# Two token tiles normalised before their transpose, and the order of the early work written as a table

## The chip, the cores and the metric

The kernel runs on one NeuronCore of a Trainium2 chip. The metric is the device time of one execution in microseconds (us). The engines work side by side and each goes through its own list of instructions in order: PE (TensorE, matmuls and transposes; PEld is its weight load), DVE (VectorE), ACT (ScalarE, activations), POOL (GpSimd) and SP (SyncE), which here issues nearly all the DMAs. An instruction that depends on another engine waits on a semaphore, and what is queued behind it on its own engine waits with it.

## The reference

The input x has 2048 tokens of 512 features, all tensors are bf16. Two residual blocks follow one another:

```
h  = x + A(layernorm(x));   out = h + B(layernorm(h))
A: q, k, v = x @ wqkv, 32 heads of 16;  phi(t) = (t + 1 if t > 0 else exp(t)) + 1e-6
   kv = sum_s phi(k) v;  z = sum_s phi(k);  o = phi(q) kv / (phi(q) z + 1e-6);  return o @ wo
B: z = gelu(x @ w_in);  z1, z2 = halves of z, 896 each;  z2 = layernorm(z2)
   g = w_sp @ z2 + b_sp   (2048 x 2048 mix over tokens);   return (z1 * g) @ w_out
layernorm(t) = (t - mean) / sqrt(var + 1e-5)
```

## The kernel before, in words

Tokens are cut into 16 tiles n = 0..15 of 128. The early stage, which the change touches, does this for each tile (lines of the profile in brackets). SP loads x[n] (L540). DVE takes mean and variance (`st`, L590, and `ag`, L594). ACT computes the reciprocal standard deviation as Ln (L605) and then Exp (L607); the groups in `LN1` (L418) share one such pair, so that tiles 2 and 3 have one pair, 4 to 7 one, and so on. The normalised tile xn[n] is written by DVE (L617) or, for tiles 5, 7, 9, 11, 13, 15, by ACT (L625). xn has to be transposed to feed the matmuls: tiles 2 and 3 go through PE (L635) and an ACT copy (L701), tiles 4 to 15 through a transposing DMA issued by SP (`tx`, L675).

Tiles 0 and 1 (`LATE`, L414) take another way. DVE subtracts only the mean into a copy `xc` (L657), PE transposes that (L686), ACT and DVE copy one half each out of PSUM (L691, L693), the k matmuls read this centred x^T (L747), and the missing factor is applied in `phi` as the scale operand of the Exp and the Relu (L716, L722). Their xn is made as well (L617), since the product xk = xn^T phi(k) reads it (L768), and a transposing DMA (L695) puts it into x^T for the q matmuls (L860).

Then `phi` of k: Exp on ACT (L716), minimum on DVE (L718), Relu on ACT (L722), sum on DVE (L724); for q, the last two are one DVE instruction (L727) that reads PSUM. PSUM has eight banks of which four hold xk until the end of the stage, so that two tiles of two banks each are left for k and q: a matmul that needs such a tile waits for the last reader of the one before. After this stage come the mixing matrix of A (to about 55 us), the output of A, the layernorm of h, z2 (L968), z1 (L1023), the token mix (L1063) and the last projection (L1083).

What sets the order: every operation is declared in `build` with `op(engine, cost, function, reads, writes, want)` and gets a number in order of declaration. `schedule` (L151) plans them with modelled costs: for each engine it takes, among the operations whose inputs are planned, the one with the smallest time plus half its `want`, from the list `WANT` (L359). The order found is the order in which the engine's instructions are emitted (`run`, L345). `fillers` (L1108) puts dummy matmuls (L578) in front of PE operations wherever the plan shows PE idle, up to the first xk. Before that, eight of them are the operation `spin` (L585).

One operation on ACT has no reader and no input: line 572, named "table".

```
op("act", (0.1, 1.3), lambda e: e.preload_act_table_set("natural_log_exp_and_others"), want=-40, name="table")
```

It loads a set of ACT's function tables by name. Nothing in the kernel loads any other set; the Gelu of line 975 has no such operation of its own.

Of the kernel before, what the change touches and what calls it, by code (L numbers as in the profile page):

```python
# [6 lines left out]
BF16 = mybir.dt.bfloat16  # L7
# [6 lines left out]
SWITCH = 0.1  # L14

# [77 lines left out]
class Program:  # L93
# [3 lines left out]
    WEIGHT = 0.5  # L97
# [53 lines left out]
    def schedule(self):  # L151

        for o in self.ops:
            o.start = None
# [5 lines left out]
        users, need = {}, {}  # L160
        for o in self.ops:
            need[o] = len(o.deps)
            for p in o.deps:
                users.setdefault(p, []).append(o)
        cand = {e: [] for e in self.ENGINES}
        for o in self.ops:
            if not need[o]:
                cand[o.eng].append(o)
        free = dict.fromkeys(self.ENGINES, 0.85)
        order = {e: [] for e in self.ENGINES}  # L170
        c_end, t_end, left, last, ring, tiling = 0.0, -9.0, len(self.ops), None, [], 0
# [21 lines left out]
        while left:  # L193
            pick = None
            for e in self.ENGINES:
                best = None
                for o in cand[e]:
                    t = free[e] + (SWITCH if e == "pe" and o.tiling != tiling else 0.0)
                    for p in o.deps:
                        t = max(t, self.ready(o, e, p))  # L200
                    ok = True
                    for tl in o.tiles:
                        if tl.slot is None:
                            s = slot(tl)
                            if s is None:
                                ok = False
                                break
                            t = max(t, s[0])
                    if ok:
                        key = (t + self.WEIGHT * o.want, o.seq)  # L210
                        if best is None or key < best[0]:
                            best = (key, o, t)
                if best is not None and (pick is None or best[2] < pick[2]):
                    pick = best
            assert pick is not None, ("no operation can go on", [(e, [(o.name, [(t.pool.name, t.width) for t in o.tiles if t.slot is None]) for o in cand[e]][:6]) for e in self.ENGINES], [(p.name, [t.ops[0].name for t in p.tiles if t.slot is not None and t.left]) for p in self.pools])
            _, o, t = pick
# [12 lines left out]
            if o.grp is not None:  # L229
                if o.nbytes < 0:  # L230
                    if len(ring) >= 3:
                        free[o.eng] = max(free[o.eng], ring[-3] - 0.3)
                    t_end = max(t + 2.2, t_end + 0.48, c_end + 0.45)
                    ring.append(t_end)
                    o.done = t_end + 0.3
                else:
                    c_end = max(t + 1.5, c_end, t_end + 1.2)
                    k = min(o.nbytes, max(0.0, 6.2 - c_end) * 250e3)
                    c_end += k / 250e3 + (o.nbytes - k) / 350e3
                    o.done = c_end + 0.4  # L240
# [7 lines left out]
            o.pos = len(order[o.eng])  # L248
# [5 lines left out]
            order[o.eng].append(o)  # L254
            cand[o.eng].remove(o)
            for u in users.get(o, ()):
                need[u] -= 1
                if not need[u]:
                    cand[u.eng].append(u)
            left -= 1  # L260
        self.order = order
# [96 lines left out]
UNIT = 0.1  # L358
WANT = [  # L359
# [37 lines left out]
]  # L397


def build(nc, A_x, A_wqkv, A_wo, B_w_in, B_w_sp, B_b_sp, B_w_out, out):  # L400
    _, S, D = A_x.shape
    F = B_w_in.shape[1]
    FH = F // 2
    H, DH = 32, D // 32
    GW = 512
    NT, KD, KF, NG = S // P, D // P, FH // P, S // GW
    TPG = GW // P
    NP = NT // 2
# [780 lines left out]
```

## Time and profile before

| | us |
|---|---|
| three timed runs | 241.86, 242.42, 245.08 (median 242.42) |
| span of the profiled execution | 240.8 |
| PE busy in the span | 235.3 |
| DVE, ACT, POOL busy | 127.1, 83.9, 13.9 |
| dummy matmuls of line 578 | 12, from 0.8 to 9.2 us |
| ACT table loads | 2, each 1.28 (at 0.79 and at 59.50) |

The profiled execution is described by its span, from its first to its last instruction. Its own time isn't listed apart; the fastest timed run lies 1.06 above that span and the median 1.62 above it. In a row of the timeline the first number is the start, the second the length, then engine, line, operation, and behind "x" how many instructions are merged into the row; the bracket tells the idle time of the engine before it and what ended it. The end of a matmul is modelled, so that rows of PE can overlap by some tenths.

### The profile page before, as it was taken

What the parts mean: (1) busy time and instruction counts of PE and PEld (TensorE: products, weight loads), DVE (VectorE), ACT (ScalarE), POOL (GpSimd) and SP (SyncE); (2) the same over time, 40 slices, a digit from 0 to 9 for tenths busy, and PEclk for the clock granted to TensorE, in tenths of its full rate; (3) what the DMA queues carried; (4) which work ended last, traced back from release to release, by engine and by line L of the source; (5) the groups of instructions that cost most, each with busy time, mean ns of one, the idle gap of its engine ahead of it and who ended that gap; (6) DMA issues with size and microseconds to landing.
All of it is one profiled execution on the core that took longest, in us unless ns stands there. A gap on an engine that the chain in (4) does not pass through costs nothing.

```text
span 240.8 us, 3056 instructions
## 1 busy us (share of the span) xinstructions
PE 235.3 (98%) x1177; PEld 108.4 (45%) x1199; DVE 127.1 (53%) x269; ACT 83.9 (35%) x132; POOL 13.9 (6%) x33
## 2 busy tenths in 40 slices
PE   8999999999999999999999999999999999999996
PEld 2434445454344544444444444444444444444443
DVE  4999856399999983226222333324333433322443
ACT  4888975566065799994111100000000000000000
POOL 3000000000102160213000000000000000000000
PEclk9999999999999999999999999999999999999999
DMA  6986559632542555444444449463300001000022
GB/s 197 254 224 91 109 114 355 207 112 81 145 125 44 92 107 101 97 88 89 109 92 104 88 92 237 108 89 88 109 0 0 25 22 44 0 3 0 0 87 87
DMA packets 61805, 24.18 MB, mean 100 GB/s; under 512 B 52064, under 2 KB 61152, under 8 KB 61792
## 3 DMA queue, kind: packets, MB, share of 16 engines
q1 hardware_dynamic: 61648, 23.97, 41.3%
q8 instruction: 9, 0.15, 0.3%
q10 hardware_dynamic: 144, 0.03, 0.1%
q14 instruction: 4, 0.03, 0.1%
HBM read 7.47 MB, written 2.10 MB: 40 GB/s over the span
## 4 chain that ended last, share of the span: by engine, by line
PE 87%; DMA 5%; DVE 3%; ACT 2%; SPq 1%; issue 1%; ACTq 0%
PE ps L1063 40%; PE ps L1083 10%; PE ps L968 10%; PE ps L1023 10%; PE ps L768 4%; PE ps L860 4%; DMA xT_pq_z<-k_xn_z 4%; PE ps L905 3%; PE ps L758 3%; PE ps L578 2%; DMA wsp<-e 1%; ACT e L716 1%; SPq L886 1%; DVE xT_pq_z L727 1%; ACT k_xn_z L836 1%
## 5 line engine op out<-in xcount | busy, mean ns | idle before, releaser
L1063 PE MATMUL ps<-wsp,k_xn_z 128*128 128x512 bf16 x328 | 73.6, 379 | 0.4
L1069 DVE TENSOR_TENSOR e<-ps,e 128x512 bf16<-128x512 f32 x28 | 19.4, 692 | 69.2 <-PE ps L1063 69.2
L1063 PEld LDWEIGHTS ps<-wsp,k_xn_z 128*128 128x128 bf16 x336 | 32.8, 98 | 39.8 <-issue 0.4
L1023 PE MATMUL ps<-hT,win 128*128 128x512 bf16 x110 | 26.0, 379 | 0.1
L968 PE MATMUL ps<-win,hT 128*128 128x384 bf16 (+1 forms) x126 | 25.3, 352 | 0.1
L1083 PE MATMUL ps<-wout,xT_pq_z 128*128 128x512 bf16 (+2 forms) x125 | 25.1, 355 | 0.1
L1063 PE MATMUL ps<-wqkv_wsp,k_xn_z 128*128 128x512 bf16 x110 | 24.2, 379 | 0.1
L1028 ACT ACTIVATE xT_pq_z<-ps 128x1024 bf16<-128x1024 f32 x14 | 14.1, 1023 | 25.6 <-PE ps L1023 25.5
L590 DVE BATCH_NORM_STATS2 small<-xh 128x6 f32<-128x512 bf16 x32 | 21.0, 679 | 3.1 <-DMA xh<-in_A_x_dram 3.0
L968 PEld LDWEIGHTS ps<-win,hT 128*128 128x128 bf16 x128 | 12.5, 98 | 12.4
L1083 PEld LDWEIGHTS ps<-wout,xT_pq_z 128*128 128x128 bf16 x126 | 11.8, 98 | 12.7
L1063 PEld LDWEIGHTS ps<-wqkv_wsp,k_xn_z 128*128 128x128 bf16 x112 | 11.0, 98 | 13.2
L1023 PEld LDWEIGHTS ps<-hT,win 128*128 128x128 bf16 x112 | 10.9, 98 | 12.7 <-DVE xh L924 0.3
L1087 DVE TENSOR_TENSOR e<-ps,xh 128x512 bf16<-128x512 f32 (+2 forms) x18 | 11.4, 633 | 9.7 <-PE ps L1083 9.2
L716 ACT ACTIVATE e<-ps 128x1024 bf16<-128x1024 f32 (+1 forms) x16 | 15.4, 973 | 2.4 <-PE ps L860 1.2
L860 PE MATMUL ps<-xT_pq_z,wqkv_wsp 128*128 128x512 bf16 x61 | 15.0, 379 | 0.6 <-DMA xT_pq_z<-k_xn_z 0.5
L768 PE MATMUL ps<-k_xn_z 128*128 128x512 bf16 x63 | 15.2, 379 | 0.2 <-issue 0.2
L975 ACT ACTIVATE k_xn_z<-ps 128x896 bf16<-128x896 f32 x12 | 10.9, 909 | 8.8 <-PE ps L968 8.8
L905 PE MATMUL ps<-k_xn_z,xT_pq_z 128*128 128x512 bf16 x58 | 13.3, 380 | 0.3 <-DVE xT_pq_z L892 0.3
L758 PE MATMUL ps<-wqkv_wsp,xT_pq_z 128*128 128x512 bf16 x55 | 13.2, 379 | 0.2 <-ACT xT_pq_z L701 0.2
L1071 DVE TENSOR_TENSOR xT_pq_z<-xT_pq_z,e 128x512 bf16<-128x512 bf16 x28 | 11.9, 425 | 2.2 <-ACT xT_pq_z L1028 1.3
L979 ACT ACTIVATE e<-k_xn_z 128x896 bf16<-128x896 bf16 x12 | 11.4, 951 | 0.3
(77 smaller groups left out, 169.4 us busy)
## 6 DMA issues: line engine op xcount, KB each, us to landing
wsp<-e SPq DMA_DIRECT2D x16, 128.0 KB
out_dram<-e SPq DMA_DIRECT2D x15, 128.0 KB, 1.7
xh<-in_A_x_dram SPq DMA_DIRECT2D x7, 256.0 KB, 3.8
win<-in_B_w_in_dram SPq DMA_DIRECT2D x1, 1792.0 KB, 7.3
wqkv_wsp<-in_A_wqkv_dram SPq DMA_DIRECT2D x3, 512.0 KB, 7.2
wout<-in_B_w_out_dram SPq DMA_DIRECT2D x1, 896.0 KB, 5.5
wsp<-in_B_w_sp_dram SPq DMA_TRANSPOSE x48, 2.6
wqkv_wsp<-in_A_wo_dram SPq DMA_DIRECT2D x1, 512.0 KB, 5.2
```

The source lines that it names most:

```text
L590: op("dve", (0.577, 0.69), lambda e: e.bn_stats(row[0:6].ap(), src.ap()), r=[src], w=[row[0:6]], want=want, name=name)
L716: first = op("act", act_c(n, ptr=len(pt)), lambda e: e.activation(e_(ev).ap(), src(t), ACT.Exp, scale=sc), r=[t()] + pt, w=[e_()], want=wa ...
L758: i = e.matmul(t(bank(ti)).ap(), lhsT=lhs.ap()[:, c, :], rhs=rhs.ap()[:, c, :], start=(c == 0), stop=(c == KD - 1))
L768: i = e.matmul(HT(bank(j)).ap(), lhsT=xn[n, j * P:(j + 1) * P].ap(), rhs=pk[n, :].ap(), start=(n == 0), stop=(n == NT - 1))
L860: k = e.matmul(t(bank(i)).ap(), lhsT=lhs.ap()[:, c, :], rhs=rhs.ap()[:, c, :], start=(c == 0), stop=(c == KD - 1))
L905: i = e.matmul(t(bank(ti)).ap(), lhsT=l.ap()[:, c, :], rhs=mw[c, :].ap(), start=(c == 0), stop=(c == KD - 1 and not unit))
L968: k = e.matmul(t(bank(i)).ap()[:, 0:b - a], lhsT=l.ap()[:, c, :], rhs=win[c, a:b].ap(), start=(c == 0), stop=(c == KD - 1))
L1023: k = e.matmul(t(bank(i)).ap(), lhsT=l.ap()[:, c, :], rhs=r_.ap()[:, c, :], start=(c == 0), stop=(c == KD - 1))
L1028: op("act", act_c(1024), lambda e: e.activation(d.ap(), t(None if same else flat).ap(), ACT.Gelu_apprx_tanh), r=[t()], w=[d], want=want + ...
L1063: k = e.matmul(t(bank(0)).ap(), lhsT=l.ap()[:, s - a, :], rhs=r_.ap()[:, s - a, :], start=(s == 0), stop=(s == NT - 1))
L1069: op("dve", dve_c(512), lambda e: e.tensor_tensor(gb().ap(), t(bank(0)).ap(), bsp().ap()[:, tg * GW:(tg + 1) * GW], ALU.add), r=[t(), bsp( ...
L1083: k = e.matmul(t(bank(0)).ap()[:, 0:r_.ap().shape[-1]], lhsT=l.ap()[:, fc, :], rhs=r_.ap()[:, fc, :], start=(fc == 0), stop=(fc == KF - 1))
```

## The change

Tiles 0 and 1 are normalised at once (subtract and multiply in one DVE instruction, as tiles 2 and 3 are), their xn is transposed on PE, and the two halves are copied by ACT and DVE straight into x^T. So the centred copies `xc` and their storage, the two transposing DMAs of line 695 and the scale operand of `phi` go. Tiles 2 and 3 get a Ln and an Exp each. The planner's choice is replaced by `ORDER`, a table with the numbers of all operations up to the mix and beyond for each engine; `schedule` now only checks that table and plans times along it. The DMA model in it has new constants; it sets nothing but the count of fillers and which buffer slot is used.

With the new numbering the operations of the first stage are: 0 to 9 loads of x0, wk, x1, x2-3, x4-5 and so on; 10 to 18 POOL's constants; 19 the table load of line 572; 20 `spin`; 21 to 40 `st`, `ag`, Ln, Exp, xn of tiles 0 to 3 (Ln 23, 28, 33, 38; Exp 24, 29, 34, 39; xn 25, 30, 35, 40); for tiles 4 to 7 Ln 49, Exp 50, xn 52 to 55; for tiles 8 to 11 Ln 64, Exp 65, minus mean 66, xn 67 to 70; 86 the load of wq; 90 and 93 transposes, 91 and 94 ACT copies, 92 and 95 DVE copies of tiles 0 and 1; 96 and 98 transposes, 97 and 99 copies of tiles 2 and 3; 100 to 111 the transposing DMAs of tiles 4 to 15; 112, 113 k of tile 0; 114 to 117 its Exp, minimum, Relu, sum; 118 its xk. The same seven for tile 1 are 119 to 125. For tiles 2 and 3, with k in one operation, they are 126 to 131 and 132 to 137; for the pair 4, 5: k 138, 139, Exp 140 to sum 143, xk 144, 145; for the pair 6, 7: k 146, 147. The first half of q of tiles 0 to 3 is 207, 208 (Exp 209, minimum 210, maximum 211), the second 212, 213 (Exp 214, 215, 216). Operation 521 is the first transposing load of w_sp.

```diff
-    def schedule(self):
+    def schedule(self, table):
+        queue = {e: [self.ops[i] for i in table[e]] for e in self.ENGINES}
...
-WANT = [
-    -66, 24, 12, 19, 28, 35, 35, 89, 106, 102, 270, 131, 15, 17, 55, 90, 42, -6, -83, 83,
...
+ORDER = {
+    "pe": [
+        20, 90, 93, 112, 113, 96, 119, 120, 98, 126, 132, 118, 207, 208, 212, 213, 125, 131, 138, 139, 137, 146,
...
+    "act": [
+        23, 24, 28, 29, 91, 33, 34, 94, 38, 39, 114, 97, 116, 99, 123, 129, 121, 49, 127, 50, 133, 135, 53, 209, 55,
+        214, 19, 64, 65, 70, 140, 142, 68, 148, 150, 233, 79, 80, 85, 164, 166, 83, 158, 156, 252, 172, 174, 180,
...
+    "dve": [
+        21, 22, 26, 25, 27, 31, 92, 30, 32, 36, 95, 37, 35, 45, 40, 47, 46, 115, 41, 117, 43, 48, 42, 44, 56, 58,
+        52, 51, 128, 60, 130, 122, 62, 124, 210, 54, 211, 63, 57, 59, 61, 134, 215, 66, 136, 216, 69, 75, 73, 77,
...
+    "sp": [
+        0, 2, 3, 1, 5, 4, 6, 86, 7, 8, 100, 101, 9, 102, 103, 107, 106, 521, 104, 105, 108, 109, 110, 111, 87, 528,
...
-    LATE = (0, 1)
+    FIRST = (0, 1)
...
-    LN1 = [[0], [1], [2, 3], [4, 5, 6, 7], [8, 9, 10, 11], [12, 13, 14, 15]]
+    LN1 = [[0], [1], [2], [3], [4, 5, 6, 7], [8, 9, 10, 11], [12, 13, 14, 15]]
...
-            if n in LATE:
-                d, m = xc[n].all(), st_x[n, 6:7]
-                cT[n] = Tile(XC)
-                op("dve", dve_f(512), lambda e, n=n, d=d, m=m: e.tensor_scalar(d.ap(), x[n, :].ap(), m.ap(), None,
-                                                                              op0=ALU.subtract),
...
-    for n in LATE:
+    for n in FIRST:
...
-                                  xc[n][c * P:(c + 1) * P].ap(), ident.all().ap())
+                                  xn[n, c * P:(c + 1) * P].ap(), ident.all().ap())
...
-        d0, d1 = xcT[n][0:2, :], xcT[n][2:4, :]
+        d0, d1 = xT[0:2, n * P:(n + 1) * P], xT[2:4, n * P:(n + 1) * P]
...
-        dma_t(xn[n, :], xT[:, n * P:(n + 1) * P], 12, f"tx{n}")
...
-        first = op("act", act_c(n, ptr=len(pt)), lambda e: e.activation(e_(ev).ap(), src(t), ACT.Exp, scale=sc),
+        first = op("act", act_c(n), lambda e: e.activation(e_(ev).ap(), src(t), ACT.Exp),
...
-            lhs = xcT[n].all() if n in LATE else xT[:, n * P:(n + 1) * P]
+            halves = ((0, 2), (2, 4)) if n in FIRST else ((0, 4),)
...
-    g.schedule()
+    g.schedule(ORDER)
```

More of the change, by code (lines that the diff above doesn't have):

```diff
@@ L14 @@
 SWITCH = 0.1
+FIRST_T = 0.8
+LAG, LAND, SHARE = 1.25, 0.45, 172e3
+RATES = [(4.0, 270e3), (11.0, 305e3), (1e9, 355e3)]
 class Store:
@@ L96 @@
     ENGINES = ("pe", "act", "dve", "pool", "sp")
-    WEIGHT = 0.5
     def __init__(self, nc):
@@ L149, in ready @@
         return p.done
-    def schedule(self):
+    def schedule(self, table):
+        queue = {e: [self.ops[i] for i in table[e]] for e in self.ENGINES}
+        assert sorted(i for e in self.ENGINES for i in table[e]) == list(range(len(self.ops)))
+        assert all(o.eng == e for e in self.ENGINES for o in queue[e])
         for o in self.ops:
@@ L159, in schedule @@
                 t.slot, t.left = None, len(t.ops)
[L160 to L171, printed above, removed]
+        free = dict.fromkeys(self.ENGINES, FIRST_T)
+        at = dict.fromkeys(self.ENGINES, 0)
+        c_end, t_end, a_beg, a_end, left, last, ring, tiling = 0.0, -9.0, 0.0, 0.0, len(self.ops), None, [], 0
         def slot(tile):
@@ L195, in schedule @@
             for e in self.ENGINES:
[L196 to L216, printed above, removed]
+                if at[e] == len(queue[e]):
+                    continue
+                o = queue[e][at[e]]
+                if any(p.start is None for p in o.deps):
+                    continue
+                t = free[e] + (SWITCH if e == "pe" and o.tiling != tiling else 0.0)
+                for p in o.deps:
+                    t = max(t, self.ready(o, e, p))
+                ok = True
+                for tl in o.tiles:
+                    if tl.slot is None:
+                        s = slot(tl)
+                        if s is None:
+                            ok = False
+                            break
+                        t = max(t, s[0])
+                if ok and (pick is None or t < pick[1]):
+                    pick = (o, t)
+            assert pick is not None, ("no operation can go on",
+                                      [queue[e][at[e]].name for e in self.ENGINES if at[e] < len(queue[e])])
+            o, t = pick
+            at[o.eng] += 1
             for tl in o.tiles:
@@ L235, in schedule @@
                     o.done = t_end + 0.3
-                else:
[L237 to L240, printed above, removed]
+                elif o.eng == "act":
+                    a_beg = max(t + LAG, a_end)
+                    a_end = a_beg + o.nbytes / SHARE
+                    o.done = a_end + LAND
+                else:
+                    c_end = max(t + LAG, c_end, t_end + 1.2)
+                    left_ = o.nbytes
+                    for until, rate in ([(a_end, SHARE)] if c_end >= a_beg - 0.3 else []) + RATES:
+                        if left_ > 0 and c_end < until:
+                            k = min(left_, (until - c_end) * rate)
+                            c_end += k / rate
+                            left_ -= k
+                    o.done = c_end + LAND
             for tl in o.tiles:
@@ L247, in schedule @@
                         tl.pool.last[c] = list(tl.ops)
-            o.pos = len(order[o.eng])
+            o.pos = at[o.eng] - 1
             if o.eng == "pool" and o.grp is None:
@@ L253, in schedule @@
                 last = o
[L254 to L259, printed above, removed]
             left -= 1
-        self.order = order
+        self.order = queue
         self.span = max(o.done for o in self.ops)
@@ L355, in run @@
                 inst.then_inc(self.sems[("eng", e)], 1)
-UNIT = 0.1
-WANT = [
[37 rows of a table removed]
-]
+ORDER = {
[10 rows of a table added]
+    ],
+    "act": [
[5 rows of a table added]
+    ],
+    "dve": [
[13 rows of a table added]
+    ],
+    "pool": [
+        14, 12, 16, 13, 17, 18, 10, 11, 15, 346, 347, 342, 343, 364, 365, 350, 351, 354, 355, 358, 359, 445, 446,
+        454, 455, 472, 473, 463, 464,
+    ],
[8 rows of a table added]
+    ],
+}
 def build(nc, A_x, A_wqkv, A_wo, B_w_in, B_w_sp, B_b_sp, B_w_out, out):
@@ L460, in build @@
     kvm = View(s_hT, KD * D * 2, [KD, P], BF16)
-    xc = [View(s_hn, 2 * i * D * 2, [D], BF16) for i in range(len(LATE))]
-    xcT = [View(s_hn, (2 * i + 1) * D * 2, [KD, P], BF16) for i in range(len(LATE))]
     at = [0]
@@ L488, in build @@
     hn_v = View(s_hn, 0, [6, D], BF16)
-    XC = g.pool("xc", len(LATE), lambda s, w: None)
-    HN = g.pool("hn", 6, lambda s, w: hn_v.ap[:, s, :], over=[XC])
+    HN = g.pool("hn", 6, lambda s, w: hn_v.ap[:, s, :])
     def sub(name, off, n, shape, dtype, over=()):
@@ L643, in T1 @@
         return 5.2 + 1.85 * n
-    rs1, cT, xn_op = {}, {}, {}
+    xn_op = {}
     for grp in LN1:
@@ L652, in build @@
         lo, hi = grp[0], grp[-1] + 1
-        for n in grp:
-            if n in LATE:
-                d, m = xc[n].all(), st_x[n, 6:7]
-                cT[n] = Tile(XC)
-                op("dve", dve_f(512), lambda e, n=n, d=d, m=m: e.tensor_scalar(d.ap(), x[n, :].ap(), m.ap(), None,
-                                                                              op0=ALU.subtract),
-                   r=[x[n, :], m], w=[d, cT[n]()], want=T1(n) - 3, name=f"xc{n}")
         rstd_act(st_x[lo:hi, 7], rs.all(), T1(lo) - 2.5, f"rs{lo}")
@@ L663, in build @@
         for i, n in enumerate(grp):
-            rs1[n] = rs[i:i + 1]
             if n in ACT_NORM1:
@@ L667, in build @@
             else:
-                xn_op[n] = normalise(xn[n, :], x[n, :], st_x[n, 6:7], rs[i:i + 1], T1(n) - 2 + 4 * (n in LATE), f"xn{n}")
+                xn_op[n] = normalise(xn[n, :], x[n, :], st_x[n, 6:7], rs[i:i + 1], T1(n) - 2, f"xn{n}")
     load("sp", "wq", wqkv[:, 0:D], w3[:, :, 0:D], D * D * 2, 27)
@@ L686, in tr0 @@
                 ins = e.transpose(t(lambda a: a[:, c // 2, :].bitcast(BF16)[:, (c % 2) * P:(c % 2 + 1) * P]).ap(),
-                                  xc[n][c * P:(c + 1) * P].ap(), ident.all().ap())
+                                  xn[n, c * P:(c + 1) * P].ap(), ident.all().ap())
             return ins
-        op("pe", pe_c(*[128] * KD), tr0, r=[xc[n].all(), ident.all(), cT[n]()], w=[t()], want=T1(n) - 1, name=f"tr{n}")
-        d0, d1 = xcT[n][0:2, :], xcT[n][2:4, :]
+        op("pe", pe_c(*[128] * KD), tr0, r=[xn[n, :], ident.all()], w=[t()], want=T1(n) - 1, name=f"tr{n}")
+        d0, d1 = xT[0:2, n * P:(n + 1) * P], xT[2:4, n * P:(n + 1) * P]
         op("act", act_c(256), lambda e, t=t, d0=d0: e.activation(d0.ap(), t(half(0)).ap(), ACT.Copy),
-           r=[t(), cT[n]()], w=[d0], want=T1(n) - 0.5, name=f"xcT{n}.0")
+           r=[t()], w=[d0], want=T1(n) - 0.5, name=f"xT{n}.0")
         op("dve", dve_2(256), lambda e, t=t, d1=d1: e.tensor_copy(d1.ap(), t(half(1)).ap()),
-           r=[t(), cT[n]()], w=[d1], want=T1(n) - 0.5, name=f"xcT{n}.1")
-        dma_t(xn[n, :], xT[:, n * P:(n + 1) * P], 12, f"tx{n}")
-    for n in range(len(LATE), NT):
+           r=[t()], w=[d1], want=T1(n) - 0.5, name=f"xT{n}.1")
+    for n in range(len(FIRST), NT):
         d = xT[:, n * P:(n + 1) * P]
@@ L704, in build, with phi @@
             dma_t(xn[n, :], d, T1(n) - 3, f"tx{n}")
-    def phi(t, w, d, src, wide, by_act, scale, want, name, after=()):
+    def phi(t, w, d, src, wide, by_act, want, name):
         n = w * GW
@@ L713, in ev @@
             return a.rearrange("p (a b) -> p a b", a=w) if wide else a
-        pt = [scale] if scale is not None else []
-        sc = scale.ap() if scale is not None else 1.0
-        first = op("act", act_c(n, ptr=len(pt)), lambda e: e.activation(e_(ev).ap(), src(t), ACT.Exp, scale=sc),
-                   r=[t()] + pt, w=[e_()], want=want, name=name + ".exp")
+        first = op("act", act_c(n), lambda e: e.activation(e_(ev).ap(), src(t), ACT.Exp),
+                   r=[t()], w=[e_()], want=want, name=name + ".exp")
         op("dve", dve_f(n), lambda e: e.tensor_scalar(e_(ev).ap(), e_(ev).ap(), 1.0, EPS_PHI, op0=ALU.min, op1=ALU.add),
@@ L721, in phi @@
             r_ = Tile(RB)
-            op("act", act_c(n, ptr=len(pt)), lambda e: e.activation(r_(ev).ap(), src(t), ACT.Relu, scale=sc),
-               r=[t()] + pt, w=[r_()], want=want, name=name + ".relu")
+            op("act", act_c(n), lambda e: e.activation(r_(ev).ap(), src(t), ACT.Relu),
+               r=[t()], w=[r_()], want=want, name=name + ".relu")
             op("dve", dve_2(n), lambda e: e.tensor_tensor(d.ap() if wide else d_flat(d), r_(ev).ap(), e_(ev).ap(), ALU.add),
@@ L740, in build, with mm @@
         for ti, n in enumerate(un):
-            lhs = xcT[n].all() if n in LATE else xT[:, n * P:(n + 1) * P]
-            for h in range(2):
-                rhs = wqkv[2 * h:2 * h + 2, D:2 * D]
-                def mm(e, t=t, ti=ti, lhs=lhs, rhs=rhs, h=h):
-                    for c in range(2):
-                        i = e.matmul(t(bank(ti)).ap(), lhsT=lhs.ap()[:, 2 * h + c, :], rhs=rhs.ap()[:, c, :],
-                                     start=(h == 0 and c == 0), stop=(h == 1 and c == 1))
-                    return i
-                if n in LATE:
-                    op("pe", pe_c(512, 512), mm, r=[xcT[n][2 * h:2 * h + 2, :], rhs, cT[n]()], w=[t()], want=T1(n),
-                       name=f"k{n}.{h}")
-            if n not in LATE:
-                rhs = wqkv[:, D:2 * D]
-                def mm(e, t=t, ti=ti, lhs=lhs, rhs=rhs):
-                    for c in range(KD):
-                        i = e.matmul(t(bank(ti)).ap(), lhsT=lhs.ap()[:, c, :], rhs=rhs.ap()[:, c, :], start=(c == 0),
-                                     stop=(c == KD - 1))
-                    return i
-                op("pe", pe_c(*[512] * 4), mm, r=[lhs, rhs], w=[t()], want=T1(n), name=f"k{n}")
+            halves = ((0, 2), (2, 4)) if n in FIRST else ((0, 4),)
+            for a, b in halves:
+                l, rhs = xT[a:b, n * P:(n + 1) * P], wqkv[a:b, D:2 * D]
+                def mm(e, t=t, ti=ti, l=l, rhs=rhs, a=a, b=b):
+                    for c in range(a, b):
+                        i = e.matmul(t(bank(ti)).ap(), lhsT=l.ap()[:, c - a, :], rhs=rhs.ap()[:, c - a, :],
+                                     start=(c == 0), stop=(c == KD - 1))
+                    return i
+                op("pe", pe_c(*[512] * (b - a)), mm, r=[l, rhs], w=[t()], want=T1(n), name=f"k{n}.{a}" if n in FIRST else f"k{n}")
         d = pk[un[0]:un[-1] + 1, :]
         src = (lambda t: t(flat).ap()) if w == 2 else (lambda t: t(bank(0)).ap())
-        phi(t, w, d, src, False, un[0] in ACT_RELU_K, rs1[un[0]] if un[0] in LATE else None, T1(un[0]) + 1, f"pk{un[0]}")
+        phi(t, w, d, src, False, un[0] in ACT_RELU_K, T1(un[0]) + 1, f"pk{un[0]}")
         for n in un:
@@ L864, in build @@
             lnexp.append(phi(t, 2, pqT[f:f + 2, gq * GW:(gq + 1) * GW], lambda t: t().ap(), True, (gq, f) in ACT_RELU_Q,
-                             None, TQ(gq) + f + 1, f"pq{gq}.{f}"))
+                             TQ(gq) + f + 1, f"pq{gq}.{f}"))
         q = pqT[:, gq * GW:(gq + 1) * GW]
@@ L1101, in build @@
     g.outs = outs
-    if WANT is not None:
-        for o, w in zip(g.ops, WANT):
-            o.want = w * UNIT
     return g
```

64 rows, old and new, of tables (ORDER, WANT) are left out of this document.

## The prediction

> **What bounds the kernel now.** I read the page first, then the busy times by stage, then the timelines of PE, ACT and DVE over the first 30 us, which the change rewrites.
>
> ```profile
> span 240.8 us, 3056 instructions
> PE 235.3 (98%) x1177; PEld 108.4 (45%) x1199; DVE 127.1 (53%) x269; ACT 83.9 (35%) x132; POOL 13.9 (6%) x33
> PE 87%; DMA 5%; DVE 3%; ACT 2%; SPq 1%; issue 1%; ACTq 0%
> ```
>
> The span is PE's work laid end to end. The stages, with the number of instructions behind each busy time, show where an engine beside PE has no room:
>
> ```profile
> 0.00:6.00 6.00, 5.15 (x15) 1.73 (x15) 2.91 (x9) 2.67 (x6) 2.01 (x13) 1.00 0.66 196
> 6.00:12.00 6.00, 5.73 (x33) 2.67 (x33) 5.99 (x20) 4.91 (x11) 0.00 (x0) 1.00 1.26 254
> 12.00:20.00 8.00, 7.44 (x35) 3.25 (x35) 7.50 (x25) 6.96 (x13) 0.00 (x0) 1.00 0.83 193
> 20.00:30.00 10.00, 9.95 (x47) 4.47 (x47) 9.07 (x21) 8.95 (x12) 0.00 (x0) 1.00 0.56 102
> ...
> 3.90:18.10 14.20, 13.35 (x65) 5.57 (x65) 13.58 (x43) 11.73 (x26) 0.00 (x0) 1.00 1.07 254
> ...
> 20.80:30.00 9.20, 9.15 (x43) 4.13 (x43) 8.27 (x20) 8.29 (x12) 0.00 (x0) 1.00 0.55 100
> 30.00:62.00 32.00, 31.31 (x225) 14.42 (x227) 21.39 (x35) 19.23 (x26) 0.96 (x2) 1.00 0.57 173
> 62.00:100.00 38.00, 37.79 (x186) 18.42 (x191) 30.18 (x73) 26.16 (x45) 7.01 (x12) 1.00 0.45 98
> ```
>
> The columns behind the window are its length, then PE, PEld, DVE and ACT busy. Three things are to be seen. From 20.80 to 100 us PE is idle for 0.05 + 0.69 + 0.21 = 0.95 us in all: a delay that PE has at 20.80 isn't made good later. In the first 20 us it is idle for 0.85 + 0.27 + 0.56 = 1.68 us, which, with the dummies below, caps what the change can win. And in 3.90 to 18.10 ACT works for 11.73 of 14.20 us: ACT can absorb 2.47 us of new work there, no more.
>
> **The change part by part.** The part that decides is the place of one instruction. In the table ACT's order begins 23, 24, 28, 29 (Ln, Exp, Ln, Exp of tiles 0 and 1), and operation 19, the table load of line 572, stands 27th, behind the second q Exp (214). In the trace of before it comes first:
>
> ```profile
> 0.79 1.28 ACT L572 ACT_TABLE_LOAD   x1 [0.79 <-PEq L1174]
> 3.91 0.30 ACT L605 ACTIVATE small<-small 128x1 f32<-128x1 f32 x1 [1.83 <-DVE small L594]
> 4.23 0.20 ACT L607 ACTIVATE small<-small 128x1 f32<-128x1 f32 x1
> ...
> 17.08 1.01 ACT L716 ACTIVATE e<-ps 128x1024 bf16<-128x1024 f32 x1
> ...
> 58.89 0.60 ACT L880 ACTIVATE e<-ps 128x512 bf16<-128x512 f32 x1
> 59.50 1.28 ACT L975 ACT_TABLE_LOAD   x1
> 67.27 0.92 ACT L975 ACTIVATE k_xn_z<-ps 128x896 bf16<-128x896 f32 x1 [6.48 <-PE ps L968]
> ```
>
> The load at 59.50 carries the line of the Gelu, and the kernel asks for none there: whoever builds the program puts a load ahead of an activation whose function isn't loaded. It starts 0.01 us after the Exp before it and doesn't sit out the 6.48 us that the Gelu waits for PE. So nothing fails when line 572 comes late; loads are put in on demand. The question is which set a Ln gets that finds none. Line 572 asks by name for a set that holds both functions. I take it that a load on demand looks at the one function at hand, as the Gelu's did, and that Ln's own set lacks Exp and the other way round. Then Ln and Exp of each group evict one another until operation 19 runs. In ACT's order up to there the ones that need a load are 23, 24, 28, 29, 33, 34, 38, 39, 49 and 127 (the Exp of tile 2's phi; 50 finds Exp loaded): ten loads. The copies, Relus and normalises between them I take to need none: in before the Square of line 979 ran under the Gelu's set with no load of its own, and the copies under the set of line 572. The first takes the place of the old one at 0.79 and is hidden by the 1.83 us wait above. Nine remain at 1.28 us each: 9 x 1.283 = 11.55 us.
>
> The mean durations for the sum, ACT first:
>
> ```profile
> L605 ACT ACTIVATE small<-small 128x1 f32<-128x1 f32 x2 | 0.6, 297 | 2.2 <-DVE small L594 2.2
> L607 ACT ACTIVATE small<-small 128x1 f32<-128x1 f32 x2 | 0.4, 204 | 0.1
> L716 ACT ACTIVATE e<-ps,small 128x512 bf16<-128x512 f32 x2 | 1.4, 690 | 0.0
> L716 ACT ACTIVATE e<-ps 128x512 bf16<-128x512 f32 x2 | 1.2, 602 | 0.0
> L572 ACT ACT_TABLE_LOAD x1 | 1.3, 1283 | 0.8 <-PEq L1174 0.8
> ...
> 7.32 0.38 DVE L617 TENSOR_SCALAR k_xn_z<-xh,small 128x512 bf16<-128x512 bf16 x1
> 17.95 0.15 DVE L621 SCALAR_TENSOR_TENSOR small<-small 128x4 f32<-128x4 f32 x1
> 18.88 0.42 DVE L724 TENSOR_TENSOR k_xn_z<-e 128x512 bf16<-128x512 bf16 x1
> 19.22 1.22 DVE L727 SCALAR_TENSOR_TENSOR xT_pq_z<-ps,e 128x1024 bf16<-128x1024 f32 x1
> ```
>
> The sum runs along ACT to the point where PE is bound again. In before, the 26 ACT instructions from 3.91 to the end of the second q Exp (17.08 + 1.01) are busy 11.73 us. In after the same stretch, Ln 23 to Exp 214, has 26 too: the pair of tiles 8 to 11 moves behind it, the new pair of tile 3 comes in. The four phi activations without a scale operand save 4 x (0.690 - 0.602) = 0.35. With nine loads ACT is always the latest engine, so its idle time vanishes, and operation 214 ends at 3.91 + 11.73 - 0.35 + 11.55 = 26.84. Then come operation 19 (1.28), Ln 64 and Exp 65 (0.30 + 0.20): 28.62. DVE has in its queue behind that Exp: minus mean 66 (0.15), the sum of tile 3 (0.42) and the maximum 216 (1.22), which frees two PSUM banks: 30.41. The same instruction ended at 19.22 + 1.22 = 20.44 before. PE's next operation, k of tiles 6 and 7, waits for these banks:
>
> ```profile
> 0.83 4.00 PE L578 MATMUL ps<-const-bfloat16-1.0 128*128 128x512 bf16 x9 [0.83 <-PEq L1174]
> 4.84 0.59 PE L686 MATMUL ps<-small,hn 128*128 128x128 bf16 x4
> 5.22 1.06 PE L578 MATMUL ps<-const-bfloat16-1.0 128*128 128x512 bf16 x2
> 6.40 0.59 PE L686 MATMUL ps<-small,hn 128*128 128x128 bf16 x4
> 6.80 1.91 PE L747 MATMUL ps<-wqkv_wsp,hn 128*128 128x512 bf16 x8
> 9.24 0.38 PE L578 MATMUL ps<-const-bfloat16-1.0 128*128 128x512 bf16 x1
> ...
> 13.04 3.61 PE L860 MATMUL ps<-xT_pq_z,wqkv_wsp 128*128 128x512 bf16 x15 [0.51 <-DMA xT_pq_z<-k_xn_z]
> 20.80 1.89 PE L758 MATMUL ps<-wqkv_wsp,xT_pq_z 128*128 128x512 bf16 x8
> ```
>
> It started at 20.80, and will at 30.8. PE's list ahead of it has the same work in both kernels (k of tiles 0 to 5, xk of 0 to 3, the four q), so this difference of 30.41 - 20.44 = 10.0 us is the loss, and PE has only those 0.95 us of idle time behind it to give any back.
>
> The rest, cheaper. The two subtractions of L657 go (their rows lie within DVE's 2.91 and 5.99 us); DVE gets no new work and waits for Exp now, so this saves nothing while ACT is late. The transposes and half copies stay, with another source and target: nothing. The two transposing DMAs of L695 go, and q no longer waits for their landing: 0.51 us of PE, inside the idle time that ACT now sets, so nothing either. If the loads were not there, it would be a gain. The Ln and Exp of tile 3 cost ACT 0.50; they are in the sum. On SP, the load of x14-15 (9) stands behind the DMA transposes 100 and 101, which wait for xn of tiles 4 and 5. xn5 ends on ACT about 24.0 (26.84 less two q Exps of 1.01 and a normalise of 0.81), so the load goes out at about 26.6 and lands 3.8 later:
>
> ```profile
> xh<-in_A_x_dram SPq DMA_DIRECT2D x7, 256.0 KB, 3.8
> 15.94 0.81 ACT L625 ACTIVATE k_xn_z<-xh,small 128x512 bf16<-128x512 bf16 x1
> 14.41 11.10 SPq L675 DMA_TRANSPOSE xT_pq_z<-k_xn_z  x8
> ```
>
> That is 30.4, when DVE comes to tile 14: nothing, and at most 1 us if one transpose more (11.10 / 8 = 1.4 us) stands before it. The load of wq (86) goes behind that of x8 but ahead of everything that waits, and is wanted at some 19 us: nothing. The early transposes of w_sp move behind operation 106; the mix is 80 us later. POOL's constants are reordered without a wait: nothing. Dummies: before has three behind the spin (1.06 + 0.38 us); the plan decides how many after has, and they run while PE waits: 0, with 1.4 us either way as bounds.
>
> PE's speed is the last unknown. The nine dummies take 0.44 us each (4.00 / 9), the eight matmuls at 6.80 0.24 (1.91 / 8), while the granted clock reads 1.00 in both stretches. In after PE idles 2 to 3 us at a time up to some 26 us. If that brings the slow speed back for 4 us on the path, 2.0 us are lost; if not, none. I take none, as most of the slow work would lie under ACT's delay.
>
> Sum: 240.8 + 10.0 = 250.8 us of span. The median of the runs stands 1.62 above the span; so the time is 242.42 + 10.0 = 252.4 us. The likeliest case by itself: 249.5 (0.95 given back, nearly 2 us of waits that I place wrongly) to 256.5 (2.0 for PE's speed, 1.0 for x14, some 0.1 us lost around each load).
>
> **The rivals.**
>
> A pause behind each load. In the row at 3.91 ACT starts 1.83 us after the load, though its releaser is DVE; so the trace allows between 0 and 1.83 us of pause. At the upper bound nine loads cost 16.5 us more: 268.9; halfway 260.7. For it speaks nothing in the rows; against it, that nothing precedes the load at 59.50. The Trainium skill, "ScalarE: Activation LUTs" (What ACT_TABLE_LOAD costs), agrees on 1283 ns and adds a drain of about 1380 ns to each switch; by that the sum would be an estimated 264.8. No row here shows that drain.
>
> No loads between Ln and Exp (the other side, not slower). If a Ln without a set gets the one for both functions, one hidden load replaces ten, and only operation 19 is left, a reload of 1.28 us at most. ACT then has room again. The change does what it says: the waits at 13.04 (0.51) and before the k of tiles 2 and 3 go, a dummy or two with them: about 241.8, between 240.5 and 243.5. For it speaks that in before Ln and Exp alternate under one set with no load between; against it, that the set has to be named. The Trainium skill, same page (Table sets: the hidden batching unit), counts one load for ln then exp, which is this case; the trace of before agrees only where the set was named. It decides from fewer than five loads: by 1.28 us each, five on the path still give 10.0 - 4 x 1.28 = 4.9 us, which is 2%.
>
> Two per cent of 242.42 are 4.85 us, about what a measurement of this kernel can tell from no change. That the order alone were over 2% slower without loads would need PE to wait for about 5 us where DVE and ACT have room; I see no such place. Faster by 2% would need more than the 1.68 + 1.44 us that PE idles or spends on dummies early, beside its start.
>
> **How the numbers follow.** Loads alternate at their bare length: 0.68. With a pause: 0.14. No loads between: 0.14, nearly all within 2%. Something else, a few loads or a slow order: 0.04, half of it over 2%. So slower 0.68 + 0.14 + 0.02 = 0.84; faster 0.01; same 0.15. The predicted time is that of the first, 252.4. The range goes from 249.0, its lower end with a little room, to 265.0, which takes in most of the pauses; it leaves out no more than 0.2.
>
> **What would show it.** ACT's groups list twelve ACT_TABLE_LOADs where there were two, most on lines of Ln and Exp before 28 us; the first k starts at about 9.5, not 6.80 (Exp of tile 1 ends at 3.91 + 2 x 0.30 + 2 x 0.20 + 3 x 1.28 = 8.75, then 0.38 for xn and 0.40 from its transpose to the k); Exp of tiles 8 to 11 ends near 28.6; k of tiles 6 and 7 starts near 30.8; PE's busy share in 6 to 28 us drops by some 10 us, and later stages only shift. I am wrong if there are two or three loads, or if pauses stand behind them.

## The result, and the profile after

The changed kernel takes 255.0 us in the median of six runs (254.76 to 255.08); the kernel before, in six runs, 242.75 us (241.86 to 245.08). The ratio is 1.0519, with a 95% interval of 1.0488 to 1.055: slower by some 5%. The forecast was 252.4 us, in a range of 249.0 to 265.0.

The page of the changed kernel:

```profile
span 253.3 us, 3085 instructions
PE 240.6 (95%) x1197; PEld 108.6 (43%) x1197; DVE 126.2 (50%) x267; ACT 96.6 (38%) x144; POOL 13.9 (5%) x33
PE 78%; ACT 12%; DMA 5%; DVE 3%; SPq 1%; issue 1%; ACTq 0%
```

ACT has 144 instructions where it had 132 and is busy for 12.7 us more; in the chain that sets the end it now has 12% where it had 2%. ACT's groups name the cause. Line 609 is the Ln, 611 the Exp, 709 the Exp of `phi`, 576 the load by name and 957 the Gelu:

```profile
L609 ACT ACT_TABLE_LOAD x5 | 6.4, 1283 | 3.9 <-DVE small L598 3.9
L611 ACT ACT_TABLE_LOAD x4 | 5.1, 1283 | 0.1
L709 ACT ACT_TABLE_LOAD x1 | 1.3, 1283 | 0.0
L576 ACT ACT_TABLE_LOAD x1 | 1.3, 1283 | 0.0
L957 ACT ACT_TABLE_LOAD x1 | 1.3, 1283 | 0.0
```

Twelve loads instead of two: the Gelu's, the named one, and ten new ones on demand, ahead of exactly the ten activations that the forecast lists. ACT's timeline:

```profile
3.87 1.28 ACT L609 ACT_TABLE_LOAD   x1 [3.87 <-DVE small L598]
5.17 0.29 ACT L609 ACTIVATE small<-small 128x1 f32<-128x1 f32 x1
5.48 1.28 ACT L611 ACT_TABLE_LOAD   x1
6.77 0.20 ACT L611 ACTIVATE small<-small 128x1 f32<-128x1 f32 x1
...
18.70 0.62 ACT L715 ACTIVATE e<-ps 128x512 bf16<-128x512 f32 x1
19.84 0.60 ACT L715 ACTIVATE e<-ps 128x512 bf16<-128x512 f32 x1 [0.52 <-PE ps L740]
...
27.84 1.01 ACT L709 ACTIVATE e<-ps 128x1024 bf16<-128x1024 f32 x1
28.87 1.28 ACT L576 ACT_TABLE_LOAD   x1
30.16 0.30 ACT L609 ACTIVATE small<-small 128x4 f32<-128x4 f32 x1
30.50 0.21 ACT L611 ACTIVATE small<-small 128x4 f32<-128x4 f32 x1
```

DVE's rows behind that last Exp, up to the maximum that frees PE's banks, follow in the order that the forecast gives:

```profile
30.73 0.16 DVE L625 SCALAR_TENSOR_TENSOR small<-small 128x4 f32<-128x4 f32 x1 [0.78 <-ACT small L611]
30.81 0.42 DVE L717 TENSOR_TENSOR k_xn_z<-e 128x512 bf16<-128x512 bf16 x1
31.15 1.22 DVE L720 SCALAR_TENSOR_TENSOR xT_pq_z<-ps,e 128x1024 bf16<-128x1024 f32 x1
```

Two more things are to be seen in ACT's rows beside the alternation. The activation behind a load starts 0.01 to 0.02 us after its end (3.87 + 1.28 = 5.15, 5.17), so there is no pause behind a load. And the first load isn't hidden: it starts at 3.87, when DVE's statistics are there, and not at 0.79. PE waits meanwhile, and its clock falls (the columns behind the window are its length, PE busy, granted clock, DMA share and GB/s; then PE's rows):

```profile
0.00:4.70 4.70, 3.87 (x9) 1.00 0.52 139
7.00:8.00 1.00, 0.43 (x5) 0.92 1.06 371
8.00:9.00 1.00, 0.36 (x1) 0.50 1.09 366
...
20.00:21.00 1.00, 1.00 (x4) 0.50 0.00 0
21.00:22.00 1.00, 1.00 (x5) 0.75 0.00 0
22.00:23.00 1.00, 1.00 (x6) 1.00 0.00 0
```

```profile
7.57 0.38 PE L682 MATMUL ps<-small,k_xn_z 128*128 128x128 bf16 x4 [2.88 <-DVE small L598]
10.60 0.61 PE L682 MATMUL ps<-small,k_xn_z 128*128 128x128 bf16 x4 [2.25 <-DVE k_xn_z L621]
11.01 1.91 PE L740 MATMUL ps<-wqkv_wsp,xT_pq_z 128*128 128x512 bf16 x4
...
25.56 1.90 PE L842 MATMUL ps<-xT_pq_z,wqkv_wsp 128*128 128x512 bf16 x8 [1.41 <-ACT e L715]
32.42 1.90 PE L740 MATMUL ps<-wqkv_wsp,xT_pq_z 128*128 128x512 bf16 x8
37.20 1.89 PE L740 MATMUL ps<-wqkv_wsp,xT_pq_z 128*128 128x512 bf16 x8 [0.29 <-DMA xT_pq_z<-k_xn_z]
```

The first k starts at 11.0 us instead of 6.80, k of tiles 6 and 7 at 32.42 instead of 20.80. These 11.6 us are nearly all of the 12.5 by which the spans differ. Some 0.4 more are lost up to a q that PE starts at 60.60 and started at 48.55 before, 0.29 of them on a transposing DMA at 37.20. The last 0.5 goes behind that, 0.16 of it in a wait for DVE at 64.41; the rest isn't followed here.

### The profile page after: what moved, and what is told of

It is laid out like the page before. It is cut to its first block, busy times and chain, and to the rows that moved or that the text cites. A ratio compares the mean times of both kernels' runs of the same rounds, so it can differ in the third digit from the quotient of the medians.

```text
span 253.3 us, 3085 instructions
## 1 busy us (share of the span) xinstructions
PE 240.6 (95%) x1197; PEld 108.6 (43%) x1197; DVE 126.2 (50%) x267; ACT 96.6 (38%) x144; POOL 13.9 (5%) x33
## 4 chain that ended last, share of the span: by engine, by line
PE 78%; ACT 12%; DMA 5%; DVE 3%; SPq 1%; issue 1%; ACTq 0%
PE ps L1045 38%; PE ps L1005 10%; PE ps L1065 10%; PE ps L950 10%; PE ps L740 4%; PE ps L887 3%; ACT L609 3%; PE ps L750 2%; DMA wsp<-e 2%; ACT e L709 2%; ACT L611 2%; DMA xT_pq_z<-k_xn_z 2%; PE ps L842 1%; SPq L868 1%; DMA xh<-in_A_x_dram 1%; DVE xT_pq_z L874 1%
## 5 line engine op out<-in xcount | busy, mean ns | idle before, releaser
L950 PE MATMUL ps<-win,hT 128*128 128x512 bf16 (+1 forms) x128 | 25.4, 352 | 0.0
L740 PE MATMUL ps<-wqkv_wsp,xT_pq_z 128*128 128x512 bf16 x64 | 18.6, 443 | 0.4 <-DMA xT_pq_z<-k_xn_z 0.3
L709 ACT ACTIVATE e<-ps 128x1024 bf16<-128x1024 f32 (+1 forms) x18 | 16.5, 926 | 4.1 <-PE ps L740 2.8
L950 PEld LDWEIGHTS ps<-win,hT 128*128 128x128 bf16 x128 | 12.5, 98 | 12.5
L1065 PEld LDWEIGHTS ps<-wout,xT_pq_z 128*128 128x128 bf16 x126 | 11.8, 98 | 12.7
L711 DVE TENSOR_SCALAR e<-e 128x1024 bf16<-128x1024 bf16 (+1 forms) x18 | 6.9, 387 | 10.4 <-ACT e L709 10.3
```

The source lines that it names most:

```text
L709: first = op("act", act_c(n), lambda e: e.activation(e_(ev).ap(), src(t), ACT.Exp), r=[t()], w=[e_()], want=want, name=name + ".exp")
L740: i = e.matmul(t(bank(ti)).ap(), lhsT=l.ap()[:, c - a, :], rhs=rhs.ap()[:, c - a, :], start=(c == 0), stop=(c == KD - 1))
L950: k = e.matmul(t(bank(i)).ap()[:, 0:b - a], lhsT=l.ap()[:, c, :], rhs=win[c, a:b].ap(), start=(c == 0), stop=(c == KD - 1))
L1065: k = e.matmul(t(bank(0)).ap()[:, 0:r_.ap().shape[-1]], lhsT=l.ap()[:, fc, :], rhs=r_.ap()[:, fc, :], start=(fc == 0), stop=(fc == KF - 1))
```

## The experiments

The loads theory says that the place of line 572 costs the time, through the loads put in on demand. The order theory, its rival, says that the new order and the normalise ahead of the transpose make PE wait by themselves. Two side questions are why the forecast was 2.6 us short and what PE's clock costs. Ratios are to the kernel before, run on the same chip (its medians there were 241.95 to 242.3 us).

**Moving the one instruction.** After planning, operation 19 is taken out of ACT's list and put back at a place i; nothing else is touched.

```diff
     fillers(g)
+    act = g.order["act"]
+    table = next(o for o in act if o.name == "table")
+    act.remove(table)
+    act.insert(i, table)
+    for i, o in enumerate(act):
+        o.pos = i
     g.waits()
```

In front (i = 0):

> The changed kernel with its table load (operation 19) moved to the front of ACT's list, all else as it is. Loads theory: two table loads are left, the named one and the Gelu's, the first Ln starts near 3.9 us, and with the other loads the whole loss goes: 241.0 to 243.0 us, best guess 241.8 (0.66 us of PE waits less than before). Order theory (the new order and the normalise ahead of the transpose make PE wait, whatever ACT loads): 252 to 255 us.

Measured: 243.15 us (241.57 to 244.62, 12 runs), ratio 1.0035 (1.0004 to 1.0066). All of the loss but 0.35% is gone with the move of one instruction, and the order theory falls. The guess of a small gain failed too: without its loads the rest of the change is no faster than before, and the time lies just above the expected range. Its profiled run, at 242.02 us below that median, has the two loads, and k of tiles 6 and 7 at 20.04, 0.76 us earlier than before.

Fifth (i = 4):

> The changed kernel with the table load fifth on ACT, behind Ln and Exp of tiles 0 and 1. Loads theory: four loads on demand and the named one, 5 x 1.28 = 6.4 us of ACT instead of 14.1, of which ACT's early idle time can take about 2.5: 3 to 5 us over the variant with the load in front, 245 to 247 us. Order theory: 252 to 255 us, no change with the place of the load.

Measured: 249.43 us (247.92 to 250.39), ratio 1.0292 (1.0255 to 1.0329). The direction is that of the loads theory, the size isn't: 6.3 us over the variant in front, not 3 to 5. PE's rows show why. First the variant with the load in front, then this one:

```profile
7.36 1.02 PE L740 MATMUL ps<-wqkv_wsp,xT_pq_z 128*128 128x512 bf16 x4 [0.55 <-ACT xT_pq_z L687]
20.04 1.89 PE L740 MATMUL ps<-wqkv_wsp,xT_pq_z 128*128 128x512 bf16 x8
```

```profile
11.95 1.89 PE L740 MATMUL ps<-wqkv_wsp,xT_pq_z 128*128 128x512 bf16 x4 [0.64 <-ACT xT_pq_z L687]
14.05 1.56 PE L740 MATMUL ps<-wqkv_wsp,xT_pq_z 128*128 128x512 bf16 x4
26.03 1.89 PE L740 MATMUL ps<-wqkv_wsp,xT_pq_z 128*128 128x512 bf16 x8
```

ACT delays the first k by 4.6 us, 1.8 less than five loads and within the 3 to 5 expected. But PE then runs k of tiles 0 and 1 at its slow speed (1.89 and 1.56 us where the quick one takes 1.02; the granted clock reads 0.50 from 12 to 15 us), and the delay has grown to 6.0 us at k of tiles 6 and 7.

Eleventh (i = 10):

> The changed kernel with the table load eleventh on ACT, behind Ln and Exp of tiles 0 to 3. Loads theory: eight loads on demand and the named one, two fewer than in the changed kernel, all on the path: 255.0 - 2 x 1.28 = 252.4 us, 251.5 to 253.2. Order theory: 255 us.

Measured: 254.39 us (253.54 to 256.36), ratio 1.0514 (1.0473 to 1.0555): hardly less than the changed kernel, although it has nine loads in place of eleven on the way. A miss; PE's clock is the suspect, and is tested below.

In the kernel before (i = 26):

> The kernel before with its table load moved behind the same 26 ACT instructions; the centred copy, the DMA transposes and the planned order stay. Loads theory: ten loads on demand and the named one, 11 x 1.28 = 14.1 us, less the 2.5 us that ACT has idle there: some 11.6 us over before, 252 to 256 us. Order theory: 242.7 us as before, or at most 3 us more.

Measured: 253.45 us (253.13 to 254.0), ratio 1.0466 (1.0438 to 1.0494), 11.2 us over before. The old data path and the old order lose nearly as much as the new ones (4.7% against 5.2%) once the load stands late. Its first load lies elsewhere:

```profile
1.12 1.28 ACT L605 ACT_TABLE_LOAD   x1 [1.12 <-POOL small L559]
3.92 0.30 ACT L605 ACTIVATE small<-small 128x1 f32<-128x1 f32 x1 [1.51 <-DVE small L594]
```

The first Ln needs two things: POOL's epsilon and DVE's variance. Here the load came behind the wait for POOL and ahead of the one for DVE. In the changed kernel it came behind the one for DVE.

**The first load.** One more load by name ahead of everything, so that the first Ln finds its own set:

```diff
+            e.preload_act_table_set("natural_log")
             g.run("act", e)
```

> The changed kernel with one more table load, of the set natural_log by name, ahead of ACT's first wait; then the first Ln should need none. In the changed kernel the first load began only at 3.87 us, when DVE's statistics were there. If that is the 1.28 us by which the forecast was short: 255.0 - 1.28 = 253.7 us, 253.2 to 254.2, and the first Ln starts near 3.9. If the other terms (PE's slow clock) take the place of that load on the path: 254.5 to 255.0.

Measured: 253.74 us (253.55 to 254.1), ratio 1.0476 (1.0453 to 1.0498): 1.26 us less than the changed kernel's 255.0. ACT's first rows:

```profile
0.79 1.28 ACT L1133 ACT_TABLE_LOAD   x1 [0.79 <-PEq L1154]
3.89 0.29 ACT L609 ACTIVATE small<-small 128x1 f32<-128x1 f32 x1 [1.82 <-DVE small L598]
4.20 1.28 ACT L611 ACT_TABLE_LOAD   x1
```

An added load makes the kernel faster by about the length of a load, since it runs at 0.79 and the first Ln starts at 3.89 instead of 5.17. The two kernels were not timed side by side: by their ratios the gain is 1.0 us, and the intervals just touch. But all four runs lie below all six of the changed kernel, and in the traces k of tiles 6 and 7 starts 1.27 us sooner (31.15 instead of 32.42). The Exp behind that Ln still needs a load, so the set natural_log serves the Ln and not the Exp.

**PE's clock.** Dummies are put ahead of PE's early operations, in the changed kernel and in the variant with the load eleventh (there 7 more ahead of k of tile 2):

```diff
     fillers(g)
+    warm = {"tr0": 11, "tr1": 8, "tr2": 8, "tr3": 8}
+    for o in g.order["pe"]:
+        if o.name in warm:
+            o.fill = warm[o.name]
```

> The changed kernel with dummy matmuls ahead of the four transposes (11, 8, 8, 8), so that PE is busy where it waited for ACT and its granted clock stays at 1.00 instead of 0.50. All table loads stay. Loads theory (ACT sets the time, the slow clock costs only the 0.5 us for which ACT waited for PE): 254.0 to 254.8 us. Clock theory (the slow clock is a large part of the 12 us): 250 to 252 us.

Measured: 254.25 us (253.81 to 256.42), ratio 1.0513 (1.0474 to 1.0551). The granted clock stays at 1.00 and k of tiles 6 and 7 starts at 31.88 instead of 32.42, so half a microsecond is there in the trace; the intervals of the times overlap, so they don't show it. That the clock is a large part of the changed kernel's loss is ruled out.

> The variant with the table load eleventh, with dummy matmuls ahead of the four transposes and of the k of tile 2 (11, 8, 8, 8, 7). In that variant PE went from 19.41 us on without a pause, at a granted clock of 0.50 up to some 22.8 us, so that 8 matmuls of k and 4 of xk took double. If that slow clock is what ate the two saved loads: 254.4 - 2.5 = 251.9 us, 251 to 253. If loads alone set the time, whatever PE's clock: 254.4.

Measured: 252.59 us (251.99 to 252.73), ratio 1.0418 (1.0391 to 1.0445): 1.8 us less than without the dummies, and the value that two loads fewer should give. PE's rows without them, and then with them:

```profile
19.41 3.59 PE L740 MATMUL ps<-wqkv_wsp,xT_pq_z 128*128 128x512 bf16 x8 [1.34 <-ACT xT_pq_z L696]
22.80 1.86 PE L750 MATMUL ps<-k_xn_z 128*128 128x512 bf16 x4
24.50 3.62 PE L842 MATMUL ps<-xT_pq_z,wqkv_wsp 128*128 128x512 bf16 x16
...
32.27 1.89 PE L740 MATMUL ps<-wqkv_wsp,xT_pq_z 128*128 128x512 bf16 x8
```

```profile
19.41 2.02 PE L740 MATMUL ps<-wqkv_wsp,xT_pq_z 128*128 128x512 bf16 x8
21.27 1.03 PE L750 MATMUL ps<-k_xn_z 128*128 128x512 bf16 x4
22.13 3.62 PE L842 MATMUL ps<-xT_pq_z,wqkv_wsp 128*128 128x512 bf16 x16
...
29.98 1.89 PE L740 MATMUL ps<-wqkv_wsp,xT_pq_z 128*128 128x512 bf16 x8
```

The same k starts at the same moment and ends 1.6 us sooner; q starts 2.4 us sooner, and k of tiles 6 and 7 2.3 us sooner. Without the dummies that k, at 32.27, comes only 0.15 us before that of the changed kernel: the slow clock took what the two loads gave. With the load eleventh ACT has no load left from 18.3 us on, and PE runs from 19.41 without a pause, so its slow clock is on the path. In the changed kernel ACT still has two loads on demand to do (20.94 and 22.55), and the slow clock lies under them. The rows without the dummies are of the run of 256.36 us, the longest of its four; there PE also waits 1.81 us for DVE at 75.79 (0.26 us at the same place with the dummies), so the two spans differ by 3.7 us.

**A better version.** The variant with the load in front, with dummies ahead of the second transpose (3 for 1) and the first k (2). The expectation also counts one ahead of the first transpose, but that one was there already: PE's first row has nine dummies in both variants, eight of `spin` and this one. So four are new:

> The variant with the table load in front, with dummies added in PE's three early pauses (1 ahead of the first transpose, 3 in place of 1 ahead of the second, 2 ahead of the first k). Its runs spread from 241.6 to 244.6 us. If that spread comes from the clock falling in the early pauses, the runs should draw together at 241.5 to 242.3, faster than before by up to 0.3%. If not: 243.1 as without them, with the same spread.

Measured: 242.14 us (241.72 to 243.08, 12 runs), ratio 1.0001 (0.9985 to 1.0018). Once more:

> The variant with the table load in front and the added dummies once more, beside the one with wk third: 242.1 us, within 0.2% of the kernel before.

Measured: 242.05 us (241.57 to 243.03, 12 runs), ratio 0.9996 (0.9972 to 1.0019). Twice the runs span 1.4 us instead of 3, with a lower median; but the time is that of the kernel before. Last, wk's load third on SP instead of fourth:

```diff
-        0, 2, 3, 1, 5, 4, 6, 86,
+        0, 2, 1, 3, 5, 4, 6, 86,
```

> The variant with the table load in front and the added dummies, with the load of wk third on SP, ahead of that of x2-3. There the first k starts at 7.02 us, though the copies of its x^T ended by 6.2: by the landing time of wk (issued at 2.17, landed some 5.0 later in the variant without the dummies) it waits for that load. If so, k of tile 0 starts near 6.5 and, if tiles 2 and 3 follow in time, 0.3 to 0.5 us go: 241.6 to 242.0 us. If x2-3, now behind 512 KB, arrives too late for the k of tile 2, the gain is lost there: 242.1 or more.

Measured: 244.48 us (243.4 to 245.98), ratio 1.0108 (1.0076 to 1.0141): slower by 1.1%, through another instruction than the k of tile 2. DVE's rows:

```profile
6.80 0.69 DVE L594 BATCH_NORM_STATS2 small<-xh 128x6 f32<-128x512 bf16 x1 [1.87 <-DMA xh<-in_A_x_dram]
7.41 0.27 DVE L689 COPY xT_pq_z<-ps 128x256 bf16<-128x256 bf16 x1
7.60 0.40 DVE L621 TENSOR_SCALAR k_xn_z<-xh,small 128x512 bf16<-128x512 bf16 x1
```

The statistics of tile 2 wait until 6.80 for x2-3, and in DVE's order the copy of tile 0's x^T and the normalise of tile 1 stand behind them. The second transpose starts at 8.06 and the first k at 8.73 instead of 7.02. Whether wk alone would have allowed an earlier start stays open.

## Why the prediction was right, and where it was short

The deciding step, that Ln and Exp evict one another's tables until operation 19 runs, is shown: by the twelve loads on the lines named, by the loss going, all but 0.35%, when the one instruction is moved (243.15 us), and by the old kernel losing 11.2 us through the same move. The Trainium skill, "ScalarE: Activation LUTs" (Table sets: the hidden batching unit), counts one load for ln then exp. That holds here only while the set for both is the active one; without it the trace shows a load at each change.

The length of a load, 1.283 us, holds. The rival of a pause behind each load falls: 0.01 to 0.02 us by the rows above. The drain of about 1380 ns that the same page (What ACT_TABLE_LOAD costs) adds to a switch isn't in this trace.

The path ran as forecast: from ACT's last Exp over DVE's three instructions to k of tiles 6 and 7. The sum was short by 2.6 us, and two of its terms carry most of that. The first is "the first takes the place of the old one at 0.79 and is hidden": it was put behind the wait for DVE and cost 1.26 us (the run with the added load). I had read from the Gelu's row that a load runs ahead of the wait; the Gelu's load did, but an activation that waits for two engines can have one of the waits ahead of its load. The second is PE's speed, "I take none": ACT waited 0.52 us for k of tiles 2 and 3. With some 0.2 us of small gaps, the second q Exp ended at 28.85 instead of 26.84.

A third term went the other way. The loss of 10.0 us is the difference of the ends of DVE's maximum, as if k of tiles 6 and 7 waited for it in both kernels. In the changed kernel it does (32.37, then 32.42); in the kernel before it started 0.36 us behind that end (20.44, then 20.80), with no wait in its row, so PE itself was the limit there. This overstated the loss by 0.3 us, and so that k, forecast at 30.8, started 1.6 later and not 2.0. Behind it another 0.9 us was lost. "PE has only those 0.95 us to give any back" held: nothing came back, and PE idles for 0.31 us from 32.4 to 40 us, where before it idled for 0.05 us in the 7.6 us from 20.80 on. PE's busy time in 6 to 28 us fell by 6.5 us (21.12 to 14.62), not by some 10, in part because matmuls at the lower clock are busy for about twice as long (1.91 against 1.02 us for four).

The steps priced at nothing behaved so in sum: with the load in front the rest of the change is worth 0.35% (0.04 to 0.66%) of loss, and with dummies nothing. Where its gain went is seen only in part. In the profiled run PE reaches the dense stretch 0.76 us earlier; the median doesn't show it, and adding dummies lowers the median by 1.0 us. That a falling clock in PE's early pauses costs the longer runs is possible, but none of them was profiled, so it isn't shown. The mean clock on record reads 1.00 for all of them but the longest (0.993), and it doesn't decide: the six runs of the changed kernel take the same time to 0.3 us, and it reads 0.973 in three of them and 1.00 in three.

## What to carry to other kernels

An instruction without readers can still have dependants: the table load had no data edge to the Ln behind it, and a list checked for completeness and data alone let it drift past 26 instructions. Where a written order replaces a planner, check first the operations whose effect is a state of the engine. Count ACT's table loads in the profile before looking at anything else, and before counting a load as hidden under a wait, find out which of the activation's waits stands ahead of the load.

## What the runs showed of the hardware

In the changed kernel the granted clock fell to 0.50 near 7.8 us, just behind one pause of PE of 2.88 us; it stayed there through shorter ones (2.25, then twice 1.08) and came back near 21.5 us, some 3.6 us after PE had become dense at 17.9. In the run with the added load it fell near 7.3 us, when PE had paused for 1.85 us, worked for 0.6 and paused for 0.4. The Trainium skill, "TensorE: Matmul & The Clock Gate" (Part 1), gives about 3.4 us for its window; the recovery agrees with that, and the two falls show that pauses shorter than a window are enough. In the first 4.7 us the clock reads 1.00 while each dummy takes 0.43 (3.87 / 9), so there the length of a matmul tells the speed and the column doesn't.
